# Attention and two MLPs on one core: issue order of VectorE and GpSimd, place of the sums, start of the weights' conversion

## The chip, the core and the metric

The kernel runs on one core of a Trainium2 chip. The metric is the device time of one execution in microseconds; three runs of the kernel before took 966.37, 964.33 and 967.18 us, with a median of 966.37 us. The trace and the page are from one profiled execution more, of 968.15 us.

## What is computed

Three layers follow one another. The first is causal attention of 4 batches and 8 heads over 576 rows of 64 values, mixed by a gate with a linear memory; the second an MLP with a squared ReLU; the third an MLP of 8 experts, one for each row.

```python
scores = where(causal, -1e9, q @ k.T / 8)
a = softmax(scores)
local = a @ v
mem_out = (phi(q) @ M_prev) / (phi(q) @ z_prev + 1e-6)
x = g * mem_out + (1 - g) * local
h = x @ w_in
x = maximum(h, 0) ** 2 @ w_out
...
out[mask] = gate_w[mask] * (maximum(x[mask] @ w1[e], 0) @ w2[e])
```

The weights w_in and w_out come as 8-byte floats. They are loaded as pairs of 32-bit integers, turned into fp32 by integer arithmetic and split into a high and a low part, so that each product is three matmuls (high by high, high by low, low by high).

## The kernel before

The attention goes over 16 pairs of heads. For each pair there are nine units in the order of ORDER: one for the last 64 rows of both heads (h is None; its scores lie in the tile A8 and come in two pieces), then four row blocks r = 3, 0, 2, 1 of each of the two heads. The loop in attention() has one turn t per unit, 144 in all with a few ahead and behind; "unit" is used for the turn too. In turn t TensorE gets, in this order, the product with v for unit t-7 (values), a half step of the MLP (step), a piece of the preparation of the next pair (prep), the transposition of unit t-4's softmax (turn) and the scores of unit t (scores). That order is fixed for TensorE over the whole attention.

scores() is a generator with five parts: the matmuls in turn t; the minimum on VectorE (L441, with the mask; minus the scores, so that it is the maximum) in turn t+1; the exponential on ScalarE (L447), in the same turn; and in turn t+2 the sums on VectorE (L450 and L451 for the unit of both heads, L455 and L456 after the second head of a row block) with the scaling on GpSimd behind them (L395 for the first pairs: a scaled identity x; L398 later: the softmax A itself). turn() then transposes with that operand. In the loop of the kernel before, `next(before)`, the sums of unit t-2, stands ahead of the first `next(here)`, the minimum of unit t-1.

later() puts work of prep(), of values() and of the MLP into a turn to come, by kind: act0 and dve0 (evacuations of PSUM), act, dve and pool (L344 and L345 for phi, L353 to L357 for the norm, L348 and L361 on GpSimd).

The weights of the first half of the MLP are converted in the same loop: 16 conversions, each a load of 512 KB into raw (L121 or L124, two buffers), an absolute value on ScalarE (L132), four steps on VectorE (L134, L135, L137, L139), the high part on ScalarE (L141) and the low part on GpSimd (L143). conversions2() gives them out in 51 steps, three to a conversion, two conversions overlapping. The table CONV says how many steps are issued by which turn: none up to turn 5, 27 by turn 43, 51 by turn 64.

step(t) begins a step of the MLP (first: 12 matmuls, L681, then ReLU, square, and the split into gh and gl with L691 on VectorE) and ends it in the next turn (second: six matmuls, L715 to L717). It begins none in a turn with t % 9 == 4, none before the rows of x are finished (rows of one batch at turn 44, of two at turn 80), and step number `at` only if min(6 * at + 9, 51) conversion steps have been issued. At the first step the four tiles of x are split (L654, L655).

The order on the other engines: manual_schedule keeps ScalarE, VectorE and GpSimd in the order of the program up to turn 9 (STRICT). From there on the framework's scheduler orders these three, and SyncE's queue always, by its own estimates; it may move an instruction ahead of others that are not ready by then.

Of the kernel before, what the change touches and what calls it, by code (L numbers as in the profile page):

```python
# [12 lines left out]
I32 = DT.int32  # L13
# [6 lines left out]
ENG = mybir.EngineType  # L20
# [34 lines left out]
XD = 4  # L55
START, EARLY, MIX = (3, 2, 1), 5, 1

STRICT, BUSY = 9, {-5: 14, 0: 12, 2: 6}


# [1 line left out]
ONPE = (NCH - 2,)  # L62
PIECES = [(5, 0), (5, 3), (5, 6), (6, 1), (6, 4)]

CONV = [(5, 0), (43, 27), (64, 51)]
CONV2 = 4.0

REST = 4
# [42 lines left out]
    return a, lo_eng.tensor_tensor(lo, src, hi.bitcast(F32), ALU.subtract)  # L111


def conversion(nc, st, sh, half, n, lo_eng, w_in, w_out):

    V = nc.vector
    raw = st.tile([128, 512, 2], I32, name="raw", tag="raw")
    f = n // 2
    f0 = half * 1024 + f * 128
    if n % 2 == 0:  # L120
        nc.sync.dma_start(raw.rearrange("p (c f) w -> p c (f w)", c=4),  # L121
                          w_in[:, f0:f0 + 128].bitcast(I32).rearrange("(c p) f -> p c f", p=128))
    else:
        nc.sync.dma_start(raw.rearrange("p f w -> p (f w)"), w_out[f0:f0 + 128].bitcast(I32))  # L124
    sl = slice((f % 2) * 512, (f % 2) * 512 + 512)
    j = f // 2 + 4 * (n % 2)
    hi, lo = sh.Wh[half][j][:, sl], sh.Wl[half][j][:, sl]
    top, low = raw[:, :, 1], raw[:, :, 0]
    yield
    t = st.tile([128, 512], I32, name="wt", tag="wt", bufs=WT)  # L130
    tf = t.bitcast(F32)
    nc.scalar.activation(tf, top.bitcast(F32), AF.Abs)  # L132
    yield
    V.tensor_scalar(tf, tf, W_LEAST, W_MOST, ALU.max, ALU.min)  # L134
    V.tensor_scalar(t, t, 3, 0x3FFFFFFF, ALU.logical_shift_left, ALU.bitwise_and)  # L135
    yield
    V.scalar_tensor_tensor(t, top, -0x40000000, t, ALU.bitwise_and, ALU.bitwise_or)  # L137
    yield
    V.scalar_tensor_tensor(t, low, 29, t, ALU.logical_shift_right, ALU.bitwise_or)  # L139
    yield  # L140
    nc.scalar.copy(hi, tf)  # L141
    yield
    lo_eng.tensor_tensor(lo, tf, hi.bitcast(F32), ALU.subtract)  # L143
    yield
# [13 lines left out]
def conversions2(*args):  # L158


    old = iter(())
    new = conversion(*args[:4], 0, *args[4:])
    next(new)
    for n in range(1, 18):
        for k in range(3):
            next(old, None)
            next(new, None)
            if k == 0 and n < 16:
                ahead = conversion(*args[:4], n, *args[4:])
                next(ahead)  # L170
            yield
        old, new = new, ahead if n < 16 else iter(())


def attention(tc, sh, q, k, v, M, z, beta, w_in, w_out, mlp, step):

    nc = tc.nc
    with ExitStack() as ctx:
# [66 lines left out]
        def mix():  # L245

            nc.scalar.activation(g_all, g_all, AF.Exp, scale=-1.0)
            nc.vector.tensor_scalar_add(gi, g_all, 1.0)
            nc.vector.reciprocal(g_all, gi)
            nc.vector.tensor_scalar(g1, g_all, -1.0, 1.0, ALU.mult, ALU.add)  # L250
            for h in range(2):
                hs = slice(h * 64, h * 64 + 64)
                nc.vector.tensor_copy(g2[hs], g1.rearrange("p (a h) -> p h a", h=2)[hs, h])
# [297 lines left out]
        def due(eng):  # L551
            for f in queue.pop((t, eng), ()):
                f()
# [8 lines left out]
        while t < len(units) + LP + 5 or queue:  # L562
            now[0] = t
            p, i = divmod(t, 9)
            if t == STRICT:
                strict.close()
            if t in BUSY:
                busy(BUSY[t])
            if t == 1:
# [5 lines left out]
                nc.scalar.copy(d, x)  # L575
            evacs.clear()
            due("act0")
            if before is not None:
                next(before)
            if here is not None:  # L580
                next(here)
            due("dve0")
            if here is not None:
                next(here)
            before, here = here, None
            if t == MIX:
                mix()
            due("act")
            due("dve")
            due("pool")  # L590
# [862 lines left out]
```

## Time and profile before

| | before |
|---|---|
| runs | 966.37, 964.33, 967.18 us |
| profiled execution | 968.15 us |
| its span, first to last instruction | 966.4 us |
| TensorE busy | 914.8 us, 95% |
| VectorE busy | 604.4 us, 63% |
| ScalarE busy | 526.2 us, 54% |
| GpSimd busy | 281.5 us, 29% |
| mean granted clock of TensorE | 0.976 |

In 40 equal slices TensorE's busy tenths are 7 to 9 in the first eight slices (24 us each) and 9 in all others but the last. Busy times are averages over stages; the attention takes the first 400 us or so, the rest of the first MLP follows, and the experts end the kernel. A matmul's end is modelled, so a busy TensorE is not one at its peak. The clock is given as a share of full speed; it has two levels, 2.4 GHz (1.0) and 1.2 GHz (0.5), so that 0.84 is a mean over a stretch.

### The profile page before, as it was taken

The numbers are of one execution on the slowest core, as the hardware profiler recorded it, in microseconds if no ns is written. First come the engines' busy times: TensorE is split into PE (matmuls) and PEld (weight loads), VectorE is DVE, ScalarE is ACT, GpSimd is POOL, SyncE is SP. The second block draws the span as 40 slices with busy tenths as digits, with TensorE's granted clock in tenths as the row PEclk, the third lists the DMA queues.
The fourth block names the chain that finished last, engine by engine and source line by source line (L and its number), as shares of the span: only waits on it lengthen the run. The fifth ranks groups of instructions, "written<-read, shape, count | busy, mean of one in ns | idle before, by whom it ended". The sixth has DMA issues, their size and how long they took to land.

```text
span 966.4 us, 19224 instructions
## 1 busy us (share of the span) xinstructions
PE 914.8 (95%) x6271; PEld 792.3 (82%) x6271; DVE 604.4 (63%) x1745; ACT 526.2 (54%) x1355; POOL 281.5 (29%) x353
## 2 busy tenths in 40 slices
PE   7987888899999999999999999999999999999993
PEld 6765766688888888899888888888899899989983
DVE  4886677656666665488616778889772535353661
ACT  3676677677666766577645555655421424242440
POOL 4453555533333443100211111333310311111111
PEclk8999999899999999999999999999999999999997
DMA  7676555454444440155220111521160634353521
GB/s 162 141 181 154 141 157 134 102 124 95 119 97 119 95 99 1 66 154 167 89 73 23 55 63 69 198 66 45 34 219 14 198 104 155 114 168 94 173 82 34
DMA packets 107081, 105.79 MB, mean 109 GB/s; under 512 B 66096, under 2 KB 76336, under 8 KB 106945
## 3 DMA queue, kind: packets, MB, share of 16 engines
q1 hardware_dynamic: 101200, 90.17, 33.6%
q0 software_dynamic: 4544, 13.67, 4.5%
q8 instruction: 65, 1.06, 0.5%
q14 instruction: 72, 0.58, 0.2%
q10 hardware_dynamic: 1200, 0.30, 0.2%
HBM read 70.80 MB, written 14.70 MB: 88 GB/s over the span
## 4 chain that ended last, share of the span: by engine, by line
PE 74%; issue 5%; DVE 3%; POOL 1%; ACT 0%; POOLq 0%; DVEq 0%
PE ps L681 20%; PE psh L1248 11%; PE y L715 7%; PE y L717 6%; PE y L716 6%; PE psy L1266 3%; PE psy L1264 3%; PE psy L1265 3%; PE xo L531 3%; PE ps L437 3%; PE pt L403 3%; DVE x L818 1%; PE xo L510 1%; PE pst L964 1%; POOL out_dram L1329 0%
## 5 line engine op out<-in xcount | busy, mean ns | idle before, releaser
L681 PE MATMUL ps<-xh,Wh 128*128 128x256 f32 x416 | 120.1, 289 | 0.0
L681 PE MATMUL ps<-xl,Wh 128*128 128x256 f32 x416 | 118.2, 284 | 1.0 <-DVE xl L655 1.0
L681 PE MATMUL ps<-xh,Wl 128*128 128x256 f32 x416 | 118.1, 284 | 0.0
L447 ACT ACTIVATE A<-A,nm 128x576 f32<-128x576 f32 (+2 forms) x144 | 84.4, 586 | 59.7 <-DVE nm L441 40.5
L715 PE MATMUL y<-Wh,gh 128*128 128x512 f32 x288 | 115.3, 400 | 0.0
L717 PE MATMUL y<-Wh,gl 128*128 128x512 f32 x288 | 113.7, 395 | 0.1
L716 PE MATMUL y<-Wl,gh 128*128 128x512 f32 x288 | 113.4, 394 | 0.0
L398 POOL TENSOR_SCALAR A<-A,sm,g 128x512 f32<-128x512 f32 (+4 forms) x108 | 74.1, 694 | 119.4 <-DVE sm L456 77.7
L1250 ACT ACTIVATE hh<-psh 128x512 fp32r<-128x512 f32 x44 | 26.4, 599 | 147.3 <-PE psh L1248 76.4
L1248 PE MATMUL psh<-xTh,Wh 128*128 128x256 f32 x352 | 100.1, 284 | 2.0 <-issue 1.3
L691 DVE TENSOR_TENSOR gl<-r,gh 128x256 fp32r<-128x256 f32 x144 | 73.8, 514 | 42.3 <-ACT gh L690 38.4
L1248 PE MATMUL psh<-xTh,Wl 128*128 128x256 f32 x352 | 99.5, 283 | 0.2 <-DVE Wl L111 0.2
L1248 PE MATMUL psh<-xTl,Wh 128*128 128x256 f32 x352 | 99.3, 282 | 0.0
L685 ACT ACTIVATE r<-ps 128x256 f32<-128x256 f32 x144 | 54.6, 379 | 74.2 <-PE ps L681 64.7
L441 DVE CUSTOM_DVE_ANT_0 A<-ps,mask 128x256 f32<-128x256 f32 (+4 forms) x160 | 75.6, 479 | 26.6 <-PE ps L437 24.7
L1251 DVE SCALAR_TENSOR_TENSOR hl<-psh,hh 128x512 fp32r<-128x512 f32 x44 | 30.4, 690 | 94.9 <-ACTq L1238 38.1
L681 PEld LDWEIGHTS ps<-xh,Wh 128*128 128x128 f32 x416 | 79.8, 192 | 4.7 <-issue 1.9
L681 PEld LDWEIGHTS ps<-xl,Wh 128*128 128x128 f32 x416 | 79.9, 192 | 3.8 <-DVE xl L655 1.2
L681 PEld LDWEIGHTS ps<-xh,Wl 128*128 128x128 f32 x416 | 79.9, 192 | 0.0
L690 ACT CAST gh<-r 128x256 fp32r<-128x256 f32 x144 | 58.4, 405 | 38.3 <-PE y L716 35.4
L1248 PEld LDWEIGHTS psh<-xTh,Wh 128*128 128x128 f32 x352 | 66.9, 190 | 4.0 <-issue 2.1
L1248 PEld LDWEIGHTS psh<-xTl,Wh 128*128 128x128 f32 x352 | 66.8, 190 | 0.7
(328 smaller groups left out, 2416.2 us busy)
## 6 DMA issues: line engine op xcount, KB each, us to landing
x<-in_moe_w_dram SPq DMA_DIRECT2D x48, 512.0 KB, 8.8
raw<-in_moe_w_in_dram SPq DMA_DIRECT2D x16, 512.0 KB, 4.7
raw<-in_moe_w_out_dram SPq DMA_DIRECT2D x16, 512.0 KB, 3.8
ks<-hk SPq DMA_DIRECT2D x60, 128.0 KB, 2.5
x2d<-x SPq DMA_DIRECT2D x18, 256.0 KB, 2.0
kn<-in_k_dram SPq DMA_DIRECT2D x32, 128.0 KB, 4.2
vn<-in_v_dram SPq DMA_DIRECT2D x32, 128.0 KB, 3.6
x2p<-x SPq DMA_DIRECT2D x16, 256.0 KB, 2.0
```

What stands on the lines that cost most here:

```text
L398: nc.gpsimd.tensor_scalar(A, A, a, b, ALU.mult, ALU.mult)
L441: nc.vector.tensor_tensor_reduce(A[:, a:a + w], tiles[j][:, :w], mask[:, end - w:end], -1.0, 3e38, ALU.add, ALU.min, nm[:, j:j + 1])
L447: nc.scalar.activation(A[:, :n], A[:, :n], AF.Exp, bias=nm[:, 0:1], scale=-1.0, accum_out=sm[:, i:i + 1])
L681: nc.tensor.matmul(ps[:, :CH], a, b, start=n == 0, stop=n == len(ops) - 1)
L685: self.later(1, "act", lambda: nc.scalar.activation(r, ps[:, :CH], AF.Relu))
L690: self.later(3, "act", lambda: nc.scalar.copy(gh, r))
L691: self.later(3, "dve", lambda: nc.vector.tensor_tensor(gl, r, gh.bitcast(F32), ALU.subtract))
L715: nc.tensor.matmul(y, gh[:, sl], wh, start=first, stop=False)
L716: nc.tensor.matmul(y, gh[:, sl], wl, start=False, stop=False)
L717: nc.tensor.matmul(y, gl[:, sl], wh, start=False, stop=last)
L1248: nc.tensor.matmul(ps[:, a], w[kc][:, sl], x[:, kc], start=kc + j == 0, stop=kc + j == 5)
L1251: nc.vector.scalar_tensor_tensor(hl, ps, 0.0, hh.bitcast(F32), ALU.max, ALU.subtract)
```

## The change

Four edits. VectorE and GpSimd stay in the program's order from turn 9 up to turn 72 (FREE); ScalarE is left to the scheduler from turn 9 as before. In the loop the sums of the unit before come behind the next unit's minimum and behind the evacuations of dve0. The conversion's first two loads are issued in turn 0, on ScalarE's queue in place of SyncE's. The table CONV runs evenly from turn 1 to 51 steps at turn 58.

```diff
+FREE = 72
 STRICT, BUSY = 9, {-5: 14, 0: 12, 2: 6}
...
-CONV = [(5, 0), (43, 27), (64, 51)]
+CONV = [(1, 0), (58, 51)]
+AHEAD = 0
...
-def conversion(nc, st, sh, half, n, lo_eng, w_in, w_out):
+def conversion(nc, st, sh, half, n, lo_eng, w_in, w_out, queue=None):
...
+    queue = queue or nc.sync
     if n % 2 == 0:
-        nc.sync.dma_start(raw.rearrange("p (c f) w -> p c (f w)", c=4),
-                          w_in[:, f0:f0 + 128].bitcast(I32).rearrange("(c p) f -> p c f", p=128))
+        queue.dma_start(raw.rearrange("p (c f) w -> p c (f w)", c=4),
+                        w_in[:, f0:f0 + 128].bitcast(I32).rearrange("(c p) f -> p c f", p=128))
     else:
-        nc.sync.dma_start(raw.rearrange("p f w -> p (f w)"), w_out[f0:f0 + 128].bitcast(I32))
+        queue.dma_start(raw.rearrange("p f w -> p (f w)"), w_out[f0:f0 + 128].bitcast(I32))
...
     old = iter(())
-    new = conversion(*args[:4], 0, *args[4:])
-    next(new)
+    nc = args[0]
+    first = [conversion(*args[:4], n, *args[4:], nc.scalar) for n in range(2)]
+    for g in first:
+        next(g)
+    new = first[0]
+    yield
     for n in range(1, 18):
         for k in range(3):
             next(old, None)
             next(new, None)
-            if k == 0 and n < 16:
+            if k == 0 and n == 1:
+                ahead = first[1]
+            elif k == 0 and n < 16:
                 ahead = conversion(*args[:4], n, *args[4:])
                 next(ahead)
             yield
...
             if t == STRICT:
                 strict.close()
+                strict.enter_context(tc.manual_schedule(engines={ENG.DVE, ENG.Pool}))
+            if t == FREE:
+                strict.close()
...
             due("act0")
-            if before is not None:
-                next(before)
             if here is not None:
                 next(here)
             due("dve0")
             if here is not None:
                 next(here)
+            if before is not None:
+                next(before)
             before, here = here, None
             if t == MIX:
                 mix()
+            if t == AHEAD:
+                next(conv)
```

How instructions move, at three places. The first is VectorE around the sums of unit 27 (wt and raw belong to a conversion, A and nm to a minimum, sm to the sums, kl to the preparation of the next pair). Before:

```order
L444 SCALAR_TENSOR_TENSOR nm<-nm 128x1
L134 TENSOR_SCALAR wt<-wt 128x512
L135 TENSOR_SCALAR wt<-wt 128x512
L137 SCALAR_TENSOR_TENSOR wt<-raw,wt 128x512
L450 SCALAR_TENSOR_TENSOR sm<-sm,mask 128x1
L139 SCALAR_TENSOR_TENSOR wt<-raw,wt 128x512
L451 RECIPROCAL sm<-sm 128x1
L296 TENSOR_TENSOR kl<-tk,hk 128x512
L441 ISA A,nm<-ps,mask 128x512
```

And with the change, where the lines have moved on by 3 to 14 (L453 is the L444 of before, L137 and L138 its L134 and L135, L140 and L142 its L137 and L139, L459 and L460 its L450 and L451, L464 and L465 its L455 and L456):

```order
L453 SCALAR_TENSOR_TENSOR nm<-nm 128x1
L464 SCALAR_TENSOR_TENSOR sm<-sm,mask 128x2
L465 RECIPROCAL sm<-sm 128x2
L140 SCALAR_TENSOR_TENSOR wt<-raw,wt 128x512
L450 ISA A,nm<-ps,mask 128x512
L450 ISA nm 128x1
L305 TENSOR_TENSOR kl<-tk,hk 128x512
L459 SCALAR_TENSOR_TENSOR sm<-sm,mask 128x1
L460 RECIPROCAL sm<-sm 128x1
L142 SCALAR_TENSOR_TENSOR wt<-raw,wt 128x512
```

A whole conversion stood between the last minimum of unit 27 and the end of its sums; now one of its steps does, with the minimum of the next unit and one evacuation.

The second place is VectorE at turns 44 and 45, where the MLP's first step begins (xl are the low parts of x that its matmuls read). Before, the last of the four splits of x stands alone, the other three having been moved far ahead:

```order
L455 SCALAR_TENSOR_TENSOR sm<-sm,mask 128x2
L441 ISA A,nm<-ps,mask 128x256
L441 ISA nm 128x1
L456 RECIPROCAL sm<-sm 128x2
L139 SCALAR_TENSOR_TENSOR wt<-raw,wt 128x512
L655 TENSOR_TENSOR xl_1544<-x_0_90,xh_1543 128x256
L441 ISA A,nm<-ps,mask 128x256
```

With the change:

```order
L137 TENSOR_SCALAR wt<-wt 128x512
L138 TENSOR_SCALAR wt<-wt 128x512
L669 TENSOR_TENSOR xl_1567<-x_0_90,xh_1566 128x256
L669 TENSOR_TENSOR xl_1571<-x_0_90,xh_1570 128x256
L669 TENSOR_TENSOR xl_1575<-x_0_90,xh_1574 128x256
L669 TENSOR_TENSOR xl_1579<-x_0_90,xh_1578 128x256
L450 ISA A,nm<-ps,mask 128x256
L450 ISA nm 128x1
L140 SCALAR_TENSOR_TENSOR wt<-raw,wt 128x512
```

The four splits now stand together ahead of the next minimum.

The third place is the start. SyncE's queue before, from the second pair's v (vn_126) on; raw is a load of weights, Mt a part of M, kn and qn are k and q of the second pair:

```order
L228 DMA vn_126<-in_v_dram 64x2x64
L233 DMA zb<-in_z_prev_dram 128x128
L121 DMA raw<-in_moe_w_in_dram 128x4x256
L232 DMA Mt_135<-in_M_prev_dram 64x64 x2
L232 DMA Mt_136<-in_M_prev_dram 64x64 x2
L124 DMA raw<-in_moe_w_out_dram 128x1024
L226 DMA kn<-in_k_dram 128x4x64 x2
L228 DMA kn<-in_k_dram 64x2x64
L226 DMA vn_127<-in_v_dram 128x4x64
L226 DMA qn<-in_q_dram 128x4x64 x2
```

SyncE's queue with the change:

```order
L237 DMA vn_126<-in_v_dram 64x2x64
L242 DMA zb<-in_z_prev_dram 128x128
L235 DMA vn_127<-in_v_dram 128x4x64 x2
L241 DMA Mt_135<-in_M_prev_dram 64x64 x2
L241 DMA Mt_136<-in_M_prev_dram 64x64 x2
L237 DMA vn_127<-in_v_dram 64x2x64
L235 DMA kn<-in_k_dram 128x4x64 x2
L237 DMA kn<-in_k_dram 64x2x64
L241 DMA Mt_137<-in_M_prev_dram 64x64 x2
L235 DMA qn<-in_q_dram 128x4x64 x2
```

And ScalarE with the change (qbh is the last copy of unit 0, A_141 its exponential):

```order
L337 CAST qs<-t_216 128x64
L340 ACTIVATE qbh<-t_216 64x64 x2
L124 DMA raw<-in_moe_w_in_dram 128x4x256
L127 DMA raw<-in_moe_w_out_dram 128x1024
L456 ACTIVATE A_141,sm<-A_141,nm 128x576
L256 ACTIVATE g_all<-g_all 128x8
```

The loads of weights left the places ahead of kn; the third pair's v, which was behind it, took them.

## Rows read from the trace of the kernel before

**Rows 1.** The whole span up to the saturated part; instructions (x) behind each busy time

```profile
core 0: us, PE busy (x) PEld busy (x) DVE busy (x) ACT busy (x) POOL busy (x), PEclk, DMA share, GB/s
0.00:180.52 180.52, 146.94 (x1028) 118.26 (x1029) 129.26 (x393) 117.22 (x321) 90.47 (x124) 0.91 0.61 148
```

**Rows 2.** The same view and columns, by nine units, from one L450 to the next

```profile
14.06:37.46 23.40, 18.35 (x116) 15.17 (x117) 13.53 (x47) 13.63 (x37) 7.31 (x11) 0.84 0.64 140
37.46:59.68 22.22, 18.78 (x138) 15.56 (x137) 20.34 (x61) 14.94 (x42) 12.88 (x16) 0.86 0.61 153
59.68:78.96 19.28, 15.98 (x136) 12.72 (x134) 15.83 (x52) 14.54 (x40) 10.22 (x13) 1.00 0.76 188
78.96:103.34 24.38, 19.21 (x134) 15.50 (x135) 15.81 (x53) 14.84 (x40) 9.37 (x13) 0.86 0.57 138
103.34:125.83 22.49, 17.34 (x140) 13.48 (x139) 15.99 (x54) 16.59 (x46) 11.96 (x13) 0.99 0.61 150
125.83:153.26 27.43, 25.77 (x180) 20.89 (x178) 19.76 (x61) 19.04 (x54) 14.02 (x14) 0.94 0.54 143
153.26:180.52 27.26, 21.15 (x141) 16.81 (x141) 22.31 (x56) 19.05 (x53) 16.72 (x19) 0.87 0.53 124
180.52:203.93 23.41, 23.41 (x179) 19.48 (x178) 12.66 (x47) 18.13 (x54) 8.73 (x11) 1.00 0.53 126
203.93:228.40 24.47, 24.47 (x188) 20.48 (x186) 13.35 (x48) 17.75 (x53) 8.76 (x11) 1.00 0.42 95
```

**Rows 3.** The chain that ended last, 190 to 220 us: start, us, what

```profile
197.85 1.44 PE ps L681 x12
...
199.75 0.23 PE y L715
```

**Rows 4.** TensorE's waits, 37.46 to 180.52 us: total us, times, longest

```profile
PE pt L405 <- POOL x L395: 6.4, 3, 2.6
```

**Rows 5.** Instructions in order of time, 76.69 to 80.57 us: start, us, what [idle before]

```profile
76.69 1.34 POOL L361 TENSOR_TENSOR e<-e,nr 128x640 f32<-128x640 f32 x1 [1.12 <-DVE nm L444]
76.95 1.36 DVE L135 TENSOR_SCALAR wt<-wt 128x512 int32<-128x512 int32 x1
78.35 0.69 DVE L137 SCALAR_TENSOR_TENSOR wt<-raw,wt 128x512 int32<-128x512 int32 x1
79.07 0.69 DVE L139 SCALAR_TENSOR_TENSOR wt<-raw,wt 128x512 int32<-128x512 int32 x1
79.68 0.16 DVE L451 RECIPROCAL sm<-sm 128x1 f32<-128x1 f32 x1
80.02 0.45 POOL L395 TENSOR_SCALAR x<-ident,sm,g 128x128 f32<-128x128 f32 x1 [1.99 <-DVE sm L451]
80.57 0.63 PE L368 MATMUL tp<-ident,e 128*128 128x128 f32 x4 [3.55 <-POOL x L395]
```

**Rows 6.** VectorE's groups, 37.46 to 125.83 us: busy us, mean ns | idle before

```profile
L137 DVE SCALAR_TENSOR_TENSOR wt<-raw,wt 128x512 int32<-128x512 int32 x9 | 8.4, 934 | 0.2
L135 DVE TENSOR_SCALAR wt<-wt 128x512 int32<-128x512 int32 x9 | 7.0, 775 | 0.1
L139 DVE SCALAR_TENSOR_TENSOR wt<-raw,wt 128x512 int32<-128x512 int32 x9 | 6.3, 701 | 0.0
L134 DVE TENSOR_SCALAR wt<-wt 128x512 f32<-128x512 f32 x9 | 4.0, 441 | 0.9 <-ACT wt L132 0.9
```

**Rows 7.** GpSimd's groups, 0 to 180.52 us: one of them

```profile
L143 POOL TENSOR_TENSOR Wl<-wt,Wh 128x512 fp32r<-128x512 f32 x16 | 21.0, 1315 | 13.7 <-ACT Wh L141 13.7
```

**Rows 8.** Instructions in order of time, SyncE at 7.86 us and TensorE at 16.80 us

```profile
7.86 0.43 SPq L121 DMA_DIRECT2D raw<-in_moe_w_in_dram  x1
...
16.80 1.09 PE L294 MATMUL tk<-ident,kn 128*128 128x128 f32 x4 [4.24 <-DMA kn<-in_k_dram]
```

**Rows 9.** VectorE's waits, 0 to 300 us

```profile
DVE gl L691 <- ACT gh L690: 4.6, 6, 1.0
```

**Rows 10.** The page's costliest groups, one of VectorE: busy us, mean ns | idle before

```profile
L691 DVE TENSOR_TENSOR gl<-r,gh 128x256 fp32r<-128x256 f32 x144 | 73.8, 514 | 42.3 <-ACT gh L690 38.4
```

## The prediction

> **What bounds the kernel now.** I read first the stretches of the whole span, then the same split by nine units, then who waits for whom there. Up to 180.52 us TensorE is busy 146.94 of 180.52 us, at a granted clock of 0.91 of its full 2.4 GHz on average [rows 1]; behind it, with the MLP's steps among the attention's work, it has no gap at all: its busy time equals the stretch, 23.41 of 23.41 us and 24.47 of 24.47 us [rows 2]. So what VectorE and GpSimd do can shorten only the first 180.52 us, which is up to unit 64 (a unit is one turn of the attention's loop, t in the code).
>
> The rows by nine units begin where VectorE adds up the sums of the small rectangles (L450), once in nine units. From the first, 14.06 us (unit 0; its sums are issued two units later), to 180.52 us (unit 63) the pace is 19.28 to 27.43 us for nine units [rows 2]. TensorE's own need is smaller. A step of the MLP is 12 matmuls of the first layer in 1.44 us and six of the second at 0.23 us each [rows 3], 2.82 us. The two saturated rows average 23.94 us with four steps in each, 11.28 us, so nine units of attention alone are 12.66 us of TensorE. Units 11 to 46, which hold a first step only at the end, took 22.22, 19.28, 24.38 and 22.49 us [rows 2], 88.37 us in place of some 53. What holds them is VectorE and the chain through it: VectorE is busy 20.34, 15.83, 15.81 and 15.99 us there, 67.97 of 88.37 us or 77%; ScalarE stands at 14.54 to 16.59 and GpSimd at 9.37 to 12.88 us a row [rows 2].
>
> The waits say how. TensorE's longest are for GpSimd's scaled operand, 6.4 us in three waits in one kind alone [rows 4]. One case can be followed: at 76.95 us a shift of the weights takes 1.36 us, the next step of the same conversion runs to 79.04 us, and the sums end at 79.84 us only after still another; GpSimd, which waited for them, starts scaling at 80.02 us, and TensorE, idle for 3.55 us, goes on at 80.57 us [rows 5]. Work that nothing needs before unit 44 stands in front of work that TensorE waits for.
>
> **The change part by part.** A conversion costs VectorE, by the means of units 11 to 46, 0.44 + 0.78 + 0.93 + 0.70 = 2.85 us [rows 6], and GpSimd 1.32 us [rows 7]. Sixteen are made, before and after; nothing is computed more or less. What changes is where.
>
> *Start, units 0 to 10 (23.40 us).* The first two loads of weights leave SyncE's queue for ScalarE's and are issued behind its copies of unit 0. ScalarE has no exponential to do then, so the two issues cost nothing as long as VectorE's first minimum stands ahead of its first exponential; without that cover about 1 us, as SyncE needs 0.43 us for one [rows 8]. SyncE does not get shorter: the third pair's v and its M move up in the place of the loads. TensorE waits 4.24 us for k of the second pair at 16.80 us [rows 8], with both loads under way already today, so I leave this wait as it is; if k lands later behind more bytes, up to 3 us more, if SyncE and ScalarE share the transfers better, up to 2 us less. VectorE is busy 13.53 of 23.40 us here and takes on about 1.7 conversions, 4.8 us, of its 9.87 idle us. Term: 0, between -2 and +3.
>
> *Units 11 to 46 (88.37 us).* 51 steps over 57 units are 0.895 a unit, three steps a conversion: 2.68 in nine units, where there were nine in 36, or 2.25. VectorE without conversions is (67.97 - 25.7)/4 = 10.6 us for nine units; with 2.68 x 2.85 = 7.6 it comes to 18.2. So its work grows by 1.2 us, and everything hangs on how well it is filled. In the new order no more than about 1.4 us of conversion stands between two minima, sums come right behind the next minimum, and each step's input was issued a unit earlier. The best rows of today fill VectorE to 82% (15.83 of 19.28) and 92% (20.34 of 22.22); today's mean is 77%. I take 87%, between the first two: 20.9 us, against 22.1. Four times -1.2 is **-4.8 us**. At 92% it is -9.2, at 77% it is +6.1.
>
> *Units 47 to 55 (27.43 us).* Four steps of the MLP are in it before and after. TensorE's need is 23.94; VectorE's 18.2 plus four subtractions of g at 0.51 us [rows 10], 20.2, fits under it at 85%. I take the middle of 23.9 and 27.4: **-1.7 us**, between -3.5 and 0.
>
> *Units 56 to 82 (27.26 + 23.41 + 24.47 = 75.14 us).* The seventh step needs 45 conversion steps issued and the eighth 51; by the old points they begin at units 59 and 64, so that units 57, 58 and 61 to 63 have none; by the new ones at 57 and 60. No more than fifteen can begin before unit 80, where the next rows of x are finished: after the change the fifteenth ends at unit 77, and 78 and 79 have none. Counted by halves, ten steps lay in this stretch and eleven do now. TensorE needs 27/9 x 12.66 = 38.0 us for the attention and 28.2 for ten steps, 66.2 us, so 8.9 us of the 75.14 are not its work; for the new load it needs 69.0. I keep a third of the 8.9, 3.0 us, and 1 us for the new hole: 73.0 us; and the step that is ahead saves 2.8 us later. Term: 73.0 - 75.1 - 2.8 = **-4.9 us**, between -8.9 and 0.
>
> *Behind unit 82* everything runs that one step ahead, and TensorE is saturated: 0.
>
> The sum is 0 - 4.8 - 1.7 - 4.9 = -11.4 us. The profiled execution took 968.15 us, of which 966.4 is its span; that makes 956.8. The runs' median of 966.37 lies 1.8 us lower, so a median of **955 us**. Fewer gaps would also mean less of the lower clock: six of the first seven rows by nine units stand at 0.84 to 0.99 [rows 2]. I count no term of its own for that.
>
> One more price is uncertain. VectorE's shift L135 takes 1.36 us at 76.95 us against a mean of 0.78; GpSimd's L361 runs from 76.69 to 78.03 us, and the shift ends 0.28 us after it [rows 5, 6]. Such hold-ups are in the means above, and by these rows the sum is the -11.4 us. In the new order a conversion's last subtraction on GpSimd (L143) and the next one's L137 on VectorE are issued in the same step, sixteen times. The Trainium skill, SBUF — State Buffer, section Who interferes with whom, says that VectorE with two inputs in SBUF, as L137 has, and GpSimd reading SBUF exclude one another for a whole instruction; by it the pairs that meet would cost more, and the sum would be that of the first rival. [...]
>
> **The rivals.** *VectorE and GpSimd collide more.* If half of the sixteen pairs collide, each by the whole 1.32 us, that is 10.5 us on VectorE over 57 units, 1.7 us in nine: 19.9 us, at 87% 22.9, so units 11 to 46 lose 3.1 instead of gaining 4.8, and the sum is about -3.5 us: **963 us**. For it: the pairs are issued together. Against: L137's mean of 0.93 shows that collisions are part of today's price, and GpSimd scales first, so the two seldom start at once.
>
> *The fixed order makes VectorE wait: slower.* In units 44 to 72 the subtraction of g (L691) and the four of x (L655) are issued in the same unit as the ScalarE copies that they read, and nothing may pass them; the next minima are queued behind. VectorE has 23.94 - 20.2 = 3.7 us to spare in nine units, or 0.9 us for each of four subtractions. Beyond that TensorE waits too. Today six of them waited 4.6 us in the first 300 us, 0.77 each [rows 9], but there the scheduler could put other work first. At some 1.8 us each, twice that, nine units lose 0.9 x 4 = 3.6 us, 28 units 11 us, and the gains of the last two terms are gone: 966.4 - 4.8 + 11 = **972 us**. It decides from 0.9 us a wait.
>
> *Nothing is gained early.* If the chain from minimum over exponential, sums and scaling to the transposition sets the pace and not VectorE's filling, units 11 to 46 stay at 22.1 us, k comes 3 us later, which takes back what is left, 3 us, of the last term: **966 us**. For it: the four rows differ in pace by 5 us at much the same busy time of VectorE.
>
> **How the numbers follow.** Forecast 0.62, with a range of its own of 946 to 961; more collisions 0.16; slower 0.14; no gain 0.08. The range leaves out the far half of the slower case and the lowest end of the bounds (966.4 - 23): **945 to 969 us**. A measurement of this kernel tells 0.3%, 2.9 us, from no change: 963.5 and 969.3. Faster: 0.62 and two thirds of the collisions, 0.74; within: 0.12; slower: 0.14.
>
> **What would show it.** In the profile of the changed kernel the stretch from the first to the sixth L450 (now L459) row should be near 107 us instead of 111.8, VectorE 85% busy in it, and no wait for GpSimd's scaled operand above 2 us. The last conversion ends near unit 58; between units 56 and 82 TensorE has no gap above 1 us except at 78. L137 with a mean above 1.3 us would show the first rival, L691 with waits above 0.9 us the second, k later than 17 us the third. Wrong is the forecast if the saturated part begins before 160 us or not before 178 us.

## The result, and the profile after

Five runs of the changed kernel took 971.44 to 974.84 us, median **972.81 us**; the kernel before 966.37 us beside it. The ratio is 1.007, 95% interval 1.005 to 1.009: slower by 0.7%, where 955 us were forecast and 969 was the upper end of the range. The profiled execution took 972.04 us, its span 970.3 us, at a granted clock of 0.976. It lies 0.8 us under its median and the one of before 1.8 us over its own, so that of the medians' 6.4 us the traces show 3.9.

The stretches by nine units again, from one sum of the unit of both heads (now L459) to the next; columns as in [rows 2]:

```profile
15.72:42.30 26.58, 21.34 (x134) 17.50 (x136) 18.46 (x55) 15.94 (x42) 11.32 (x13) 0.81 0.63 159
42.30:63.84 21.54, 15.72 (x125) 13.38 (x122) 18.88 (x57) 14.93 (x40) 12.01 (x14) 0.92 0.61 143
63.84:87.18 23.34, 17.65 (x135) 14.24 (x134) 17.99 (x55) 15.63 (x43) 12.81 (x14) 0.93 0.66 167
87.18:110.03 22.85, 18.24 (x133) 14.86 (x131) 17.66 (x55) 15.64 (x42) 11.92 (x13) 0.85 0.64 166
110.03:140.03 30.00, 19.61 (x144) 16.14 (x142) 20.76 (x58) 16.82 (x47) 14.16 (x14) 0.83 0.51 129
140.03:167.14 27.11, 24.43 (x179) 19.25 (x178) 19.46 (x57) 19.35 (x56) 15.92 (x16) 1.00 0.52 123
167.14:191.42 24.28, 24.24 (x183) 20.05 (x182) 14.57 (x51) 18.83 (x57) 12.61 (x15) 1.00 0.42 93
191.42:213.84 22.42, 22.42 (x176) 18.83 (x175) 11.11 (x45) 15.59 (x49) 9.36 (x11) 1.00 0.48 119
213.84:235.41 21.57, 21.57 (x166) 17.54 (x165) 13.72 (x48) 16.78 (x52) 9.32 (x11) 1.00 0.48 108
```

| stretch | before, us | forecast of the difference | after, us | difference |
|---|---|---|---|---|
| to the first of these sums | 14.06 | 0 (with the next line) | 15.72 | +1.66 |
| units 2 to 10 | 23.40 | | 26.58 | +3.18 |
| units 11 to 37 | 65.88 | -4.8 (with the next line) | 67.73 | +1.85 |
| units 38 to 46 | 22.49 | | 30.00 | +7.51 |
| units 47 to 55 | 27.43 | -1.7 | 27.11 | -0.32 |
| units 56 to 82 | 75.14 | -2.1 | 68.27 | -6.87 |
| the rest of the span | 738.0 | -2.8 | 734.9 | -3.1 |

The late gain came, and larger than forecast; the start and units 38 to 46 took it back. Three places show how. The start, from the timeline of all engines (ACTq and SPq are DMA issues on ScalarE's and SyncE's queues):

```profile
7.92 0.45 ACT L340 ACTIVATE qbh<-t 64x64 fp32r<-64x64 f32 x2
...
11.81 0.38 ACTq L124 DMA_DIRECT2D raw<-in_moe_w_in_dram  x1
12.03 1.10 SPq L235 DMA_DIRECT2D kn<-in_k_dram  x2
12.69 0.35 ACTq L127 DMA_DIRECT2D raw<-in_moe_w_out_dram  x1
13.09 0.77 ACT L456 ACTIVATE A<-A,nm 128x576 f32<-128x576 f32 x1 [4.71 <-DMA Mt<-in_M_prev_dram]
...
18.42 0.45 PE L303 MATMUL tk<-ident,kn 128*128 128x128 f32 x1 [5.79 <-DMA kn<-in_k_dram]
```

ScalarE is done at 8.37 us, but its first load goes out at 11.81. It waited for a small transfer of M on SyncE's queue, data that the load has nothing to do with. The program's own list of waits shows the tie: the transfers of SyncE's and ScalarE's queues take eight completion counters (DMAHW0 to DMAHW7) in turn, and each waits for the transfer that used its counter before.

```
ScalarE  L124 DMA raw<-in_moe_w_in_dram 128x4x256 [waits DMAHW0_49]
SyncE    L241 DMA Mt_135<-in_M_prev_dram 64x64 [waits DMAHW0_49,Pool_49]
```

The first exponential is queued behind it: 13.09 us. Before, it had only VectorE's minimum to wait for:

```profile
12.06 0.77 ACT L447 ACTIVATE A<-A,nm 128x576 f32<-128x576 f32 x1 [3.75 <-DVE nm L444]
```

And the two loads, 1 MB, now leave together with k of the second pair; TensorE has it at 18.42 us, not at 16.80 [rows 8].

The first step of the MLP, at turn 44, from the engines' timelines:

```profile
120.64 0.28 PE L695 MATMUL ps<-xh,Wh 128*128 128x256 f32 x1
123.49 1.53 POOL L357 TENSOR_TENSOR u<-e,zb 128x640 f32<-128x640 f32 x1 [2.09 <-DMA kn<-in_k_dram]
124.98 1.27 POOL L146 TENSOR_TENSOR Wl<-wt,Wh 128x512 fp32r<-128x512 f32 x1
125.06 0.82 DVE L362 TENSOR_REDUCE nr<-u 128x10 f32<-128x640 f32 x1 [1.42 <-POOL u L357]
126.28 0.67 ACT L135 ACTIVATE wt<-raw 128x512 f32<-128x512 f32 x1 [2.10 <-POOL Wl L146]
126.98 0.83 DVE L137 TENSOR_SCALAR wt<-wt 128x512 f32<-128x512 f32 x1 [0.46 <-ACT wt L135]
127.85 1.36 DVE L138 TENSOR_SCALAR wt<-wt 128x512 int32<-128x512 int32 x1
129.13 2.49 DVE L669 TENSOR_TENSOR xl<-x,xh 128x256 fp32r<-128x256 f32 x4
130.66 0.58 PE L695 MATMUL ps<-xl,Wh 128*128 128x256 f32 x1 [9.74 <-DVE xl L669]
```

TensorE has issued the first matmul of the step and waits 9.74 us for the second one's operand. Before, all its waits for xl in units 38 to 46 were this one:

```profile
PE ps L681 <- DVE xl L655: 1.0, 1, 1.0
```

With the change the four splits of x stand in VectorE's fixed order behind a norm that waits for GpSimd's u and a conversion that waits for ScalarE, which waits for GpSimd. None of that concerns x. The clock falls in the gap; by 1-us windows (columns as in [rows 2]) it is at the lower level from 126 into the window of 135 us, after TensorE had done nothing since 120.92, so that the step's first twelve matmuls run at half rate:

```profile
120.00:121.00 1.00, 0.92 (x11) 0.65 (x7) 1.00 (x2) 0.21 (x1) 1.00 (x1) 1.00 0.97 236
126.00:127.00 1.00, 0.00 (x0) 0.00 (x0) 0.50 (x3) 0.67 (x1) 1.00 (x3) 0.50 0.56 129
134.00:135.00 1.00, 1.00 (x7) 1.00 (x6) 0.73 (x3) 1.00 (x4) 0.00 (x0) 0.50 0.00 0
136.00:137.00 1.00, 1.00 (x10) 1.00 (x10) 0.93 (x8) 0.18 (x1) 0.00 (x0) 1.00 0.00 0
```

Last, turn 16, from the timeline of all engines. TensorE's wait at its end comes back in each of the next two pairs (4.01, 3.50 and 2.81 us):

```profile
51.15 0.56 DVE L450 CUSTOM_DVE_ANT_0 A<-ps,mask 128x384 f32<-128x384 f32 x1 [1.14 <-PE ps L446]
51.63 0.75 DVE L553 COPY x<-xo 128x256 f32<-128x256 f32 x2
52.43 0.45 DVE L346 SCALAR_TENSOR_TENSOR qbl<-t,qbh 64x64 fp32r<-64x64 f32 x2
52.91 0.50 DVE L353 TENSOR_SCALAR e<-e 128x640 f32<-128x640 f32 x1
53.44 0.82 DVE L354 SCALAR_TENSOR_TENSOR e<-qn,e 128x640 f32<-128x640 f32 x1
54.18 0.69 DVE L142 SCALAR_TENSOR_TENSOR wt<-raw,wt 128x512 int32<-128x512 int32 x1
54.58 1.69 POOL L357 TENSOR_TENSOR u<-e,zb 128x640 f32<-128x640 f32 x1 [2.57 <-DMA kn<-in_k_dram]
54.90 0.42 DVE L450 CUSTOM_DVE_ANT_0 A<-ps,mask 128x256 f32<-128x256 f32 x1
55.25 1.03 DVE L464 SCALAR_TENSOR_TENSOR sm<-sm,mask 128x2 f32<-128x2 f32 x1
57.19 0.58 PE L414 MATMUL pt<-x,A 128*128 128x128 f32 x1 [4.01 <-POOL x L404]
```

Between two minima VectorE is busy for 3.2 us: copies of x, the tail's splits, phi, and one step of the conversion. Only then come the minimum, the sums, GpSimd's scaling, and TensorE. In the next pairs phi stands one turn ahead of the copies. These waits for the scaled operand are what the edit of the sums was to shorten. In units 11 to 37 TensorE had four of them, 9.9 us (the three of [rows 4] and the first line here); with the change it has four again, 12.0 us:

```profile
PE tp L368 <- POOL x L395: 3.5, 1, 3.5
PE pt L414 <- POOL x L404: 12.0, 4, 4.0
```

### The profile page after: what moved, and what is told of

Same layout as the page of the kernel before. It is cut to its first block, busy times and chain, and to the rows that moved or that the text cites. A ratio compares the mean times of both kernels' runs of the same rounds, so it can differ in the third digit from the quotient of the medians.

```text
span 970.3 us, 19203 instructions
## 1 busy us (share of the span) xinstructions
PE 910.7 (94%) x6271; PEld 789.9 (81%) x6271; DVE 605.5 (62%) x1745; ACT 525.5 (54%) x1355; POOL 292.1 (30%) x353
## 4 chain that ended last, share of the span: by engine, by line
PE 72%; DVE 9%; issue 6%; DMA 4%; ACT 3%; POOL 2%; SPq 1%; POOLq 0%; ACTq 0%; DVEq 0%
PE ps L695 17%; PE psh L1262 11%; PE y L729 5%; PE y L731 5%; PE y L730 5%; PE ps L446 5%; PE xo L540 4%; PE pt L412 4%; PE psy L1280 3%; PE psy L1278 3%; PE psy L1279 3%; DMA kn<-in_k_dram 2%; DMA raw<-in_moe_w_out_dram 1%; PE pt L414 1%; DVE x L832 1%
## 5 line engine op out<-in xcount | busy, mean ns | idle before, releaser
L407 POOL TENSOR_SCALAR A<-A,sm,g 128x512 f32<-128x512 f32 (+4 forms) x108 | 77.4, 724 | 131.1 <-DVE sm L465 89.2
L456 ACT ACTIVATE A<-A,nm 128x576 f32<-128x576 f32 (+2 forms) x144 | 84.6, 587 | 50.1 <-DVE nm L450 29.6
L450 DVE CUSTOM_DVE_ANT_0 A<-ps,mask 128x256 f32<-128x256 f32 (+4 forms) x160 | 75.6, 479 | 54.0 <-PE ps L446 52.7
L705 DVE TENSOR_TENSOR gl<-r,gh 128x256 fp32r<-128x256 f32 x144 | 69.0, 480 | 41.5 <-ACT gh L704 36.4
L1278 PE MATMUL psy<-Wh,hh 128*128 128x512 f32 x168 | 67.0, 399 | 0.1
```

The source lines that it names most:

```text
L407: nc.gpsimd.tensor_scalar(A, A, a, b, ALU.mult, ALU.mult)
L450: nc.vector.tensor_tensor_reduce(A[:, a:a + w], tiles[j][:, :w], mask[:, end - w:end], -1.0, 3e38, ALU.add, ALU.min, nm[:, j:j + 1])
L456: nc.scalar.activation(A[:, :n], A[:, :n], AF.Exp, bias=nm[:, 0:1], scale=-1.0, accum_out=sm[:, i:i + 1])
L705: self.later(3, "dve", lambda: nc.vector.tensor_tensor(gl, r, gh.bitcast(F32), ALU.subtract))
L1278: nc.tensor.matmul(y[h], xh, wh, start=g + a == 0, stop=False)
```

## The experiments

Five rounds each, the kernel before beside them (965.4 to 966.2 us). S is the fixed order, U the sums behind the minimum, C the table, Q the two loads on ScalarE's queue.

| | kernel | median, us | ratio to before, 95% |
|---|---|---|---|
| 1 | change + x split early | 974.82 | 1.0101 (1.0077 to 1.0125) |
| 2 | change - Q | 970.0 | 1.0045 (1.0027 to 1.0063) |
| 3 | change - Q + x split early | 972.65 | 1.0077 (1.0059 to 1.0095) |
| 4 | change - S | 967.18 | 1.0012 (1.0001 to 1.0023) |
| 5 | before + U + C | 965.25 | 0.9994 (0.998 to 1.0007) |
| 6 | before + C | 961.45 | 0.9948 (0.9932 to 0.9964) |
| 7 | change - U | 975.14 | 1.011 (1.0074 to 1.0146) |
| 8 | change - C | 983.92 | 1.018 (1.0154 to 1.0207) |
| 9 | change + x split early, light turns | 968.19 | 1.0036 (1.002 to 1.0053) |
| 10 | change, S to turn 40 | 966.26 | 1.0006 (0.9991 to 1.002) |
| 11 | before + table even from 5 | 966.48 | 1.0011 (0.9995 to 1.0027) |
| 12 | before + table even from 11 | 967.39 | 1.0027 (1.0006 to 1.0047) |
| 13 | change, the two loads in turn 1 | 974.26 | 1.0085 (1.0064 to 1.0107) |
| 14 | change - Q, S to turn 40 | 960.39 | 0.9942 (0.9922 to 0.9961) |
| 15 | before + U | 966.85 | 1.0013 (1.0 to 1.0025) |
| 16 | as 14, phi and norm a turn later | 974.75 | 1.008 (1.0059 to 1.0102) |

**Runs 1 and 3, x split early.** In values(), where a quarter of x is copied out; the split at turn 44 goes. Run 3 is this and run 2 together.

```diff
                     later(1, put[0], lambda d=..., x=...: put[1](d, x))
+                    if cc == 0:
+                        mlp.split_piece(hp)
...
+        self.later(1, "act", lambda: nc.scalar.copy(a, x))
+        self.later(1, "dve", lambda: nc.vector.tensor_tensor(b, x, a.bitcast(F32), ALU.subtract))
```

> The changed kernel with one thing added: each quarter of the first rows of x is split in the turn in which it is finished (turns 16, 25, 34 and 43) in place of all four together at turn 44. Theory A (the loss is the start, and one block: four splits of x that stand in VectorE's fixed order behind a norm and a conversion that wait): TensorE's single wait of 9.7 us for xl shrinks to 2.5 us or less, units 38 to 46 take 22.5 to 25 us in place of 30.0, and the time is 965 to 968.5 us against 972.8. Rival B (the fixed order makes VectorE late there whatever stands in it): another wait takes its place, units 38 to 46 stay above 27.5 us, and the time is 971 to 974 us.

> Both edits of the two kernels before together: x split early, and the two loads on SyncE's queue. Theory A: the two losses add, and with both gone the gains of the earlier conversion remain: 960 to 964 us, below the kernel before (966.4). Rival (both losses hide behind something common, such as units that run faster when they come later): 966 to 970 us.

Theory A fell in both: by the medians 2.0 and 2.7 us slower than without the early splits. The 9.7 us were gone and units 38 to 46 took 26.75 us, but in this profile (3.6 us above the run's median) units 11 to 37 took 5.8 us more; in run 3, whose profile lies at its median, 5.1 us more than in run 2 (71.86 and 66.79 us). The split now stands in the full turn, behind a copy of ScalarE in the same turn, and the wait of 4.01 us there is 5.24 (the three such waits add up to 12.9 us in place of 10.3, so they are not the whole 5.8):

```profile
54.50 0.43 DVE L660 TENSOR_TENSOR xl<-x,xh 128x256 fp32r<-128x256 f32 x1 [0.93 <-ACT xh L659]
...
59.12 0.58 PE L414 MATMUL pt<-x,A 128*128 128x128 f32 x1 [5.24 <-POOL x L404]
```

**Runs 9 and 10, the splits elsewhere.** Run 9 against run 1, and run 10 against the change:

```diff
-        self.later(1, "act", lambda: nc.scalar.copy(a, x))
-        self.later(1, "dve", lambda: nc.vector.tensor_tensor(b, x, a.bitcast(F32), ALU.subtract))
+        self.later(3 if kc < 3 else 1, "act", lambda: nc.scalar.copy(a, x))
+        self.later(4 if kc < 3 else 1, "dve", lambda: nc.vector.tensor_tensor(b, x, a.bitcast(F32), ALU.subtract))
...
-FREE = 72
+FREE = 40
```

> The changed kernel with each quarter of x split early, as in the first of these runs, but three to four turns after it is finished (turns 19, 28 and 37; the last at turn 43) in place of the very turn in which VectorE also copies x out of PSUM. That run took the wait of 9.7 us away and was 2 us slower than the changed kernel, with 5.8 us more in units 11 to 37. Theory A3 (in the fixed order a split costs what the turn has no room for; the turn of the x copies is the fullest): units 11 to 37 come back to 67 to 69 us in place of 73.6, units 38 to 46 stay at 25 to 27, and the time is 967 to 970 us. Rival (in the fixed order any addition before unit 44 costs as much as the block at 44 did): units 11 to 37 above 71 us, time 972 to 976 us.

> The changed kernel with the fixed order of VectorE and GpSimd ended at turn 40 in place of 72, ahead of the first step of the MLP; the scheduler then puts three of the four splits of x into places left in units 11 to 40. Theory A3 (what the fixed order costs is the first step of the MLP alone): units 11 to 37 67 to 69 us, 38 to 46 23 to 26 us, no wait for xl above 2 us; 966 to 969 us, as with the scheduler from turn 9. Rival (the splits placed into the fixed stretch cost there what they cost in the first of these runs): units 11 to 37 above 71 us and the time 971 to 975 us.

Both times are as theory A3 had it: 6.6 us better than run 1 for three subtractions moved by three turns, with their copies on ScalarE moved by two, and 6.5 us better than the change with the order ended ahead of turn 44. Units 11 to 37 are 66.26 and 67.09 us, the wait of turn 16 back at 4.00 and 4.21 us. In run 9 units 38 to 46 still take 26.67 us; in run 10 TensorE waits 0.3 us for xl, and the stretch that had 30.00 us reads

```profile
109.74:130.27 20.53, 17.38 (x138) 13.40 (x138) 17.70 (x54) 15.89 (x45) 13.71 (x13) 1.00 0.70 161
```

**Runs 2, 4, 7 and 8, one edit undone each,** in this order:

```diff
-    first = [conversion(*args[:4], n, *args[4:], nc.scalar) for n in range(2)]
...
+    new = conversion(*args[:4], 0, *args[4:])
+    next(new)
...
-            if t == AHEAD:
-                next(conv)
...
-                strict.enter_context(tc.manual_schedule(engines={ENG.DVE, ENG.Pool}))
...
             due("act0")
+            if before is not None:
+                next(before)
             if here is not None:
...
-CONV = [(1, 0), (58, 51)]
+CONV = [(5, 0), (43, 27), (64, 51)]
```

> The changed kernel without its edit of the queue: the first two loads of weights are issued on SyncE's queue, ahead of k of the second pair, as before; the conversion still begins at turn 1. Theory A (moving the two loads to ScalarE's queue delayed ScalarE's first exponential and k of the second pair): the first sums start at 14.1 us in place of 15.7, TensorE's wait for k ends at 16.8 to 17.2 in place of 18.4, the first nine units take 23.4 to 24.5 us in place of 26.6, and the time is 967.5 to 970 us against 972.8. Rival C (the early conversion, in VectorE's order there and through its raw loads, is what slows the start): the first nine units stay at 26 us or more, and the time is 971 to 974 us.

> The changed kernel without its fixed order: VectorE and GpSimd are given to the scheduler from turn 9, as before; the other three edits stay. Its order has the first splits of x far ahead again, with one alone at turn 44. Theory A: no wait of TensorE for xl above 2 us, units 38 to 46 below 25 us; the start stays as in the changed kernel, first sums at 15.7 us; time 965 to 969 us. Rival B (the fixed order itself costs in units 11 to 37 as well): units 11 to 37 fall from 67.7 to 64 us or less, and the time is below 964 us. Rival D (the fixed order is what makes the conversion early enough for the gain in units 56 to 82): that gain goes, the three rows from unit 56 on take over 72 us in place of 68.3, and the time stays above 970 us.

> The changed kernel with the sums ahead of the next unit's minimum again, in the fixed order. TensorE's waits for GpSimd's scaled operand, 14.2 us in five in the changed kernel, end with the sums. If the sums' place sets them: each shrinks by about one minimum (0.5 us) and the time is 969.5 to 971.5 us. Rival (ahead of the minimum VectorE waits for the exponential and every minimum gets late; the sums' waits for ScalarE are already 8.0 us in nine): units 11 to 37 above 70 us and the time 975 to 981 us. If neither: 972 to 974 us.

> The changed kernel with the old table of the conversion. Theory A2: the first nine units go back to 23.5 to 24.5 us, the wait for xl at the first step stays above 4 us, and the gain of units 56 to 82 goes (73 to 76 us there in place of 68.3): 975 to 979 us. Rival (the table gives nothing by itself, its gain is made by the fixed order): the gain stays, and the time is 968 to 971 us.

Q costs 2.8 us here: first exponential at 11.73 us, k at 16.43. Units 2 to 10 stayed at 26.10 us, though: without Q the table alone lengthens them by 2.7 us. In run 8, with Q and without the table, they take 25.90. So either edit lengthens this stretch, and both together (26.58) hardly more than one. S costs 5.6 us, and the trace puts it in units 38 to 46 (22.72 us in place of 30.00); units 11 to 37 take 67.85 us without it and 67.73 with it. U: the intervals of run 7 and the change overlap, and its waits for the scaled operand are about as long (3.99 and 3.93 us the longest), so its time tells nothing. The traces do tell one price of U: in each of the thirteen profiles with it TensorE waits once, between 31 and 37 us, 2.1 to 2.6 us for the scaled operand; in the five without it (before and runs 6, 7, 11 and 12) no such wait there is longer than 0.2 us. C is worth 11 us inside the change, more than the 2 to 6 us forecast for run 8; without it units 47 to 82 take 109.4 us, 95.4 with it. The start did not become shorter, against theory A2.

**Runs 5, 6, 11, 12 and 15, the edits on the kernel before.** `CONV = [(1, 0), (58, 51)]` is all of run 6; 11 and 12 put (5, 0) and (11, 0) in the place of (1, 0).

> The kernel before with two of the four edits, the sums behind the next minimum and the even table (the changed kernel without the fixed order and with the two loads on SyncE's queue). Theory A2 (the queue of the two loads costs 1.3 to 1.8 us at the start, the early conversion 2.5 to 3 us in units 2 to 10, the fixed order some 7 us at the first step of the MLP, and the earlier table gives 8 to 9 us back from unit 56 on): the costs of the order and of the queue are gone, first sums at 14.0 to 14.4 us, 963.5 to 966 us. Rival (the scheduler arranges the start anew and takes the cost of the early conversion away too): first nine units 23.4 to 24 us and 960.5 to 963 us.

> The kernel before with the even table alone. Theory A2: where the scheduler orders VectorE, the place of the sums in the program matters little: within 1.5 us of the run with both edits, 963 to 966.5 us, with 26 us for the first nine units and below 71 us for units 56 to 82 (75.1 before). Rival (the sums' place is what holds or frees TensorE): more than 2 us from it, above 968 or below 961 us.

> The kernel before with a table that is even from turn 5 to 58: 51 steps in 53 turns. The even table from turn 1, alone, gave 961.45 us, with 3.2 us lost in the first nine units and 2.8 in units 11 to 46, and 5.6 us gained in units 56 to 82. Theory A3 (the loss at the start is VectorE's work there): the first nine units take 24.5 to 26 us in place of 26.6, the gain behind unit 55 stays, units 11 to 46 lose up to 1 us more: 960 to 962.5 us. Rival (the pace of units 2 to 46 is set by other waits, so that the table's start does not matter): the first nine units at 26 us or more, 961.5 to 965 us.

> The same, even from turn 11 to 58: 51 steps in 47 turns, 1.09 a turn, so that the first nine units hold no step at all. Theory A3: the first nine units 23.4 to 24.5 us, and units 11 to 46 up to 2 us longer than the 91.2 us of the table from turn 1, as VectorE's load there grows by 13%: 959.5 to 962.5 us. Rival (units 11 to 46 are so full that each step moved into them costs its own time, 1.1 conversions of 2.85 us for each nine units more): units 11 to 46 above 95 us and 964 us or more.

> The kernel before with the sums behind the next minimum as the only edit. With the even table the scheduler's kernel was 3.8 us slower with this edit than without it (965.25 and 961.45), while in the fixed order the edit saved 2.3 us. If the later sums cost under the scheduler as such: 967.5 to 971 us. If the 3.8 us are particular to that pair of kernels: 964 to 967 us.

The table alone is faster than both kernels, 961.45 us. Its profile has units 56 to 82 at 69.51 us (75.14 before), and loses 3.2 us in units 2 to 10 and 2.8 in units 11 to 46. Theory A2 had 963 to 966.5 us for it and missed: with U beside the table 3.8 us of its gain are gone, while U alone costs at most 0.25%; where these 3.8 us go is open. Run 11 is a miss that teaches: in its profile (963.03 us) units 2 to 10 take 22.33 us, shorter still than theory A3 had it, but that was the fastest of twelve runs that went up to 969.16, and the median is 5 us worse than the table from 1. Run 12 missed too: the order of SyncE's loads changed with it (TensorE waits 3.59 and 2.81 us for q), and the scheduler put eight steps of the conversion into units 2 to 10, which were to hold none; so it doesn't tell.

**Run 13, the loads a turn later.**

```diff
-AHEAD = 0
+AHEAD = 1
```

> The changed kernel with its first two loads of weights still on ScalarE's queue, but issued in turn 1, behind the first unit's exponential, in place of turn 0; SyncE's order stays that of the changed kernel. In seven profiles with the loads on ScalarE's queue at turn 0 the first exponential starts at 13.0 to 13.4 us and TensorE's wait for the second pair's k or q ends at 18.3 to 19.7; in seven without it 11.7 to 12.4 and 15.3 to 17.2. Theory Q1 (ScalarE stands still before the two issues, and the load's 1 MB moves at the same time as k): the exponential is back at 11.7 to 12.5, k at 15.3 to 17.2, and the time 969 to 971 us. Rival Q2 (SyncE's order, with the third pair's v and M ahead of k, makes k late): the exponential is back, k still ends at 18 us or later, and the time is 971 to 973 us. Rival Q3 (the loads now stand before the next exponentials and wait for a transfer there): the second unit's exponential later than 16.5 us, time 973 us or more.

```profile
12.70 0.78 ACT L456 ACTIVATE A<-A,nm 128x576 f32<-128x576 f32 x1 [3.75 <-DVE nm L453]
14.66 0.39 ACTq L124 DMA_DIRECT2D raw<-in_moe_w_in_dram  x1
15.30 0.63 PE L303 MATMUL tk<-ident,kn 128*128 128x128 f32 x4 [2.11 <-DMA kn<-in_k_dram]
16.50 0.72 ACT L456 ACTIVATE A<-A,nm 128x512 f32<-128x512 f32 x1 [2.84 <-DVE nm L450]
22.30 0.45 PE L309 MATMUL tq<-ident,qn 128*128 128x128 f32 x1 [5.82 <-DMA qn<-in_q_dram]
```

SyncE's order is the change's, and k is there at 15.30: Q2 is out. Q1 was right for k and close for the exponential (12.70), but not for the time: what moves beside the loads is late, now q, for which TensorE waits 5.82 us. The second unit's exponential, at 16.50, comes 0.66 us later than in the change, close to what Q3 had; it stands behind the second load's issue, but the profile names VectorE's minimum as what it waited for, so Q3 is not settled. The Trainium skill, DMA: Bandwidth & Descriptors, section Issuing engines are not separate DMA queues, says that transfers issued by different engines run on the same DMA engines and interleave. This trace agrees: the two large pieces of q, issued from 15.33 us on beside the two loads, took 5.1 us to land (median); in run 2, with the loads ahead on SyncE's queue, 3.3 us.

**Run 14, both losses away** (the edits of runs 2 and 10).

> The changed kernel with the fixed order ended at turn 40 and the two loads on SyncE's queue: of the change the sums behind the minimum, the even table and the fixed order of units 9 to 40 are left. Ending the order at 40 took 6.5 us off, the loads on SyncE's queue 2.8. If the two add: 963 to 965 us, below the kernel before (965.5 in the last call). If what is left of the first nine units is set by something common: 965.5 to 968 us.

They add, and more: 960.39 us, below the 963 to 965 expected. Against run 10, from which it differs in the loads' place alone, that place is worth 5.9 us; in the change it was 2.8. Why is open. Run 6, the table alone, is as fast (the intervals overlap), so nothing here shows a gain of the other three edits over the table. By the profile of run 14, against [rows 2]:

```profile
14.45:40.80 26.35, 21.64 (x135) 17.88 (x136) 18.33 (x57) 16.05 (x42) 11.27 (x13) 0.81 0.66 158
...
108.57:128.62 20.05, 16.50 (x135) 12.78 (x133) 17.83 (x54) 15.43 (x45) 13.50 (x13) 1.00 0.62 150
128.62:154.65 26.03, 24.69 (x182) 20.13 (x182) 19.84 (x58) 18.77 (x54) 14.67 (x18) 1.00 0.58 143
154.65:178.12 23.47, 22.68 (x174) 18.66 (x174) 14.48 (x50) 18.03 (x56) 11.14 (x14) 1.00 0.46 103
```

**Run 16, phi a turn later,** on run 14. It changes what is computed: phi then reads q behind the load of the next pair's.

```diff
-            later(1, "dve", phi)
+            later(2 if p else 1, "dve", phi)
...
-            later(1, "dve", norm)
+            later(2 if p else 1, "dve", norm)
```

GpSimd's two products behind them move in the same way.

> The kernel of the run before last (fixed order to turn 40, loads on SyncE's queue, 960.39 us), with the preparation's phi (two steps on VectorE, 1.3 us) and the norm, and GpSimd's two products behind them, one turn later from the second pair on. Theory A4 (TensorE's waits for the scaled operand, 4.2, 3.7 and 3.0 us once in each pair, come from the turn in which phi, the copies of x, the tail's splits and a step of the conversion all stand ahead of one minimum): each of these waits falls by 1 us or more, units 11 to 37 take 62 to 65.5 us in place of 67.8, and the time is 956 to 959.5 us. Rival (phi then stands ahead of the next minimum and the same wait appears one turn later): the waits in sum stay, 959.5 to 962 us. Rival (the norm or e now comes too late for its transposition): a new wait of TensorE for e or for pT, 962 us or more.

It fell. Only in turn 16 did phi leave the copies of x (wait 3.83 us for 4.20). In the next pairs it now joined them: 6.21 us for 3.70, 6.92 for 3.00; within the last VectorE also waits 2.32 us for the load of q that the edit put ahead of phi.

```profile
77.53 0.75 DVE L547 COPY x<-xo 128x256 f32<-128x256 f32 x2
78.20 0.48 DVE L347 TENSOR_SCALAR e<-e 128x640 f32<-128x640 f32 x1
...
83.38 1.31 POOL L398 TENSOR_SCALAR x<-ident,sm,g 128x128 f32<-128x128 f32 x2
84.31 0.58 PE L408 MATMUL pt<-x,A 128*128 128x128 f32 x1 [6.21 <-POOL x L398]
```

So the wait grew where more was put into that turn; a version that empties it in all pairs was not tried, and theory A4 stays unproven.

## Why the prediction was wrong

*What bounds the kernel.* Right for TensorE behind 180 us. Wrong for units 11 to 46: "everything hangs on how well it is filled". VectorE came out 88%, 77%, 77% and 69% busy, not 87%, and TensorE's waits for the scaled operand did not fall below 2 us: in units 11 to 37 they are 12.0 us, 9.9 before. The step that failed counted only "no more than about 1.4 us of conversion" between two minima. That held at turn 16 (0.69 us), but copies of x, the tail's splits and phi stand there too, 3.2 us in all, and the sums now wait behind them with the minimum. By the places shown, the pace is set by single turns in which VectorE is too full, or in which its fixed order waits, and by the clock behind them; that no other place counts as much was not tested.

*Start, forecast 0.* The step "the two issues cost nothing as long as VectorE's first minimum stands ahead" failed: I looked at what ScalarE had to do and not at what the issue itself waits for. "I leave this wait as it is" failed too. The whole start measured +4.8 us, outside the term's own -2 to +3. In the seven profiles with Q in turn 0 the first exponential starts at 13.0 to 13.4 us and TensorE's work on the second pair's k at 18.3 to 19.7; in the ten with these loads on SyncE's queue, before included, at 11.5 to 12.4 and 15.3 to 17.2. And the 4.8 us of conversion were not free in VectorE's idle time: with the table from turn 1 and the loads on SyncE's queue (runs 2, 3, 5, 6, 14) units 2 to 10 hold ten steps of it on VectorE and take 24.85 to 26.57 us; before and in runs 11 and 15, with three or four steps there, 22.33 to 23.80.

*Units 11 to 46, forecast -4.8, measured +9.4.* 7.5 us of it lie in units 38 to 46, where TensorE waits for the four splits. They stood in the instruction lists, and the second rival named them, with 0.9 to 1.8 us a wait and a price from waits of the free order [rows 9]; the sum held nothing for them. Here a wait in the fixed order cost what all the waiting work ahead of it added up to, 9.74 us. Without that block (run 14) these units take 87.82 us, 0.5 less than before: nearly nothing is gained there, as the third rival said, with units 11 to 37 1.9 us longer and units 38 to 46 2.4 us shorter.

*Units 47 to 55, forecast -1.7:* -0.3; in run 14 -1.4.

*Units 56 to 82, forecast -2.1, and -2.8 behind:* right in kind, too small: -6.9 and -3.1. I kept a third of the 8.9 us of TensorE's gaps; all of them went, and the three rows show TensorE busy for 68.23 of 68.27 us.

*Collisions:* L140, one of a conversion's four steps on VectorE, has a mean of 0.73 us in units 11 to 46, the same step before 0.93 [rows 6], and the four together 2.72, 2.85 before; the first rival is out. The slower rival's 972 us was the right number, but partly by luck: of the two things it named only x waited, and L705 (L691 before) shows no wait before 180 us; the late gains, which it wrote off, came, and the start, which it did not name, took them back. (By the prediction's own terms, faster and within add up to 0.73 and 0.13, not 0.74 and 0.12.)

The forecast's sum needed a kernel without the two losses: run 14 gains 5.0 us by the medians where 11.4 were forecast, all of it behind unit 37.

## What to carry to other kernels

Before fixing an engine's order, read the list for each place where something that the bottleneck needs stands behind work that waits for a third engine; ending the fixed order ahead of such a place gave 6.5 us back (run 10 against the change). What the fixed order is worth ahead of that place is not settled: run 14 has it and is 4.9 us faster than run 5, which has not; but run 6, with the table alone, has neither it nor U and is as fast. So try each edit alone before joining them. Spread work by turns, not by averages: three subtractions of 0.4 us, moved by three turns with their copies, were worth 6.6 us. And a DMA moved to an idle engine's queue brings its waits along, and its bytes still meet those of the others.

## What the runs showed of the hardware

VectorE's sums of 128x2, which read sm and mask in SBUF, took 1.03 us at 55.25 us where most others take 0.14 to 0.16; they end at 56.28 us, GpSimd's u at 56.27. The Trainium skill, SBUF — State Buffer, section Who interferes with whom, says that a VectorE instruction with two inputs in SBUF contends with a GpSimd instruction that reads SBUF; this row agrees.

The ten runs of run 6 spread with the granted clock, from 959.95 us at 0.987 to 964.52 us at 0.981; elsewhere this is looser (run 11 has 965.17 and 969.16 us, both at 0.982). One profile can lie 3.1 to 3.6 us off its median, on either side (runs 1, 6 and 11), which is as much as some edits here are worth.
